# One kernel, four edits: score banks for the last two tiles, a transpose through VectorE and DRAM, a bank order, one clamp

## The chip, the cores and the metric

The kernel is one launch on one core of a Trainium2 chip. The metric is the device time of that launch in microseconds (us), lower is better. The core has five engines that run their own instruction queues in order and wait for each other through semaphores: TensorE (PE, matmuls, with its weight loads listed as PEld), VectorE (DVE), ScalarE (ACT), GpSimd (POOL) and SyncE (SP, which here issues every DMA; its queue is listed as SPq).

## The reference

Attention over pooled queries, then two mixing layers, all in f32:

```
q_pool = mean of neighbouring query rows          # 1152 -> 576 rows, 4 batches x 8 heads, 64 wide
attn   = softmax(q_pool @ k.T / 8);  x = attn @ v  # x: 4 x 576 x 512
xk, xr = mu * x + (1 - mu) * x_prev                # first mixing layer
x      = sigmoid(xr @ w_r) * (relu(xk @ w_k)**2 @ w_v)
theta  = x @ w_theta                               # second mixing layer
y      = w_tok_r @ (x * cos(theta)) + w_tok_i @ (x * sin(theta))
u      = x + y
out    = u + relu(u @ w_ch)
```

A matmul of f32 operands is done in three passes on two rounded parts of each operand (high by high, high by low, low by high; `PASS`). The parts are cut out by ACT (the high one) and by DVE or POOL (the low one).

## The kernel before, in words

The program has three stages, and the order of the instructions on each engine is written out by hand: functions are hung on slots or ticks, and a tick is called after a fixed piece of PE work.

**Attention.** 16 pairs of heads, 9 tiles of 128 query rows each, 144 tiles. A tile's scores fill a set of three PSUM banks; two such sets (`SC`, named sc) take turns. DVE takes the row maximum, ACT the exponential, and then the 128x1152 result must be turned so that keys lie on partitions. For four of nine tiles DVE and DMAs do that; for the others PE transposes nine blocks (`fill`, line 396): one into the third bank of the tile's own scores, four into the bank TX (tx) and four into TY (ty). ACT and DVE copy them out (`take`, line 407). Tiles 7 and 8 of the last pair are the last of the stage and are of that kind. The product with v follows (line 430).

**First mixing layer.** Tokens of all batches are worked in eight halves of 288. `gate` (line 812), `hidden` (line 843) and `value` (line 862) are runs of 48, 96 and 96 matmuls; the gates are done three halves ahead of the others. The shifted inputs are prepared by ACT (line 780), DVE (line 785) and POOL or DVE (line 792). The last five pieces of w_v are converted from f64 while the stage runs (`late_v`, lines 970 to 982): line 970 is the absolute value on ACT, line 972 the clamp on POOL, lines 976 to 978 the bits on DVE, line 982 the low part. `LATE_TICKS` gives for each piece the ticks of its three steps. The results of a matmul run go to PSUM banks in turn; from hidden(6) on, the list `LB` sets which of six banks are taken, starting inside the list where the running count stands: at index 3, which is bank 3, then 5, 7, 0 and so on. `value(5)` has just used banks 4 to 7, and DVE empties them in line 868.

**Second mixing layer.** Tokens are cut into 18 groups of 128 (`angles`; batches 0 and 2 have five, and the fifth holds the last 64 tokens of two batches). Of each group n, `ysplit` (ACT line 1037, POOL line 1038) cuts the two parts of x, `theta(n)` (line 1089) multiplies with w_theta, DVE reduces the angle (lines 1095 to 1104, the last being a clip), ACT makes cosine and sine (1107 to 1109), and `mult` (line 1119, lines 1079 and 1080 for the fifth group) multiplies them with x. For that product x is needed with tokens on partitions, while it is kept with channels on partitions. `turn(n)` makes it: four PE transposes into bank 6 (line 1047) and two ACT copies into the tiles t (line 1050). It is called from `prepare`, inside theta(n-1), four ticks ahead. The products are cut again (lines 1070, 1071) and feed `mix` (line 1143, 108 matmuls per half of 288 tokens), whose result goes through lines 1148, 1150 and 1151 to `final` (line 1162, 48 matmuls). The thetas of batch b+1 are put between the matmuls of mix and final of batch b, at the places of `TPOS`.

Of the kernel before, what the change touches and what calls it, by code (L numbers as in the profile page):

```python
# [11 lines left out]
F32 = mybir.dt.float32  # L12
# [3 lines left out]
ALU = mybir.AluOpType  # L16
# [12 lines left out]
HALF = 288  # L29
WARM = 16  # L30
THIRDS = 6
AHEAD = 3
SHIFT = 33
TURN = 4
TPOS = ((1, 0), (1, 3), (2, 0), (3, 0), (3, 3))
THETA = (1, 2, 4, 5)
YM = (1, 0)
YL = 1
YS = 2
LB = (0, 1, 2, 3, 5, 7)  # L40
PACE = 2.5

CLO = 'pool'
# [4 lines left out]

PIECES = {"a": ((1, 2), ((3, 2), (3, 2), (3, 2)), (9, 2), 14, 15), "x": ((1, 2), ((3, 2), (3, 2), (3, 2)), (4, 2), 6, 7)}
LATE = 5  # L50
LATE_TICKS = ((15, 16, 17), (18, 19, 20), (11, 24, 25), (13, 26, 27), (21, 28, 29))

F64_MIN = float(np.array([0x38000000], np.uint32).view(np.float32)[0])
F64_MAX = float(np.array([0x47EFFFFF], np.uint32).view(np.float32)[0])
# [8 lines left out]
def attn_moe_kernel(ctx: ExitStack, tc: tile.TileContext, qT, kT, vP, muk, mur, wk, wv, wr, wth, wtr, wti, wch, ident, out):  # L63
    nc = tc.nc
    pe, act, dve, pool, sp = nc.tensor, nc.scalar, nc.vector, nc.gpsimd, nc.sync
# [3 lines left out]
    dram = ctx.enter_context(tc.tile_pool(name="dram", bufs=2, space=DRAM))  # L69

    idn = const.tile([128, 128], F32, name="idn")
# [9 lines left out]
    XT = [big.tile([128, 4, 577 + 63 * (1 - b % 2)], F32, name=f"xt{b}") for b in range(NB)]  # L81
# [76 lines left out]
    def attention(first):  # L158
# [11 lines left out]
        TX = psV.tile([128, 512], F32, tag="tx", name="tx")  # L170
# [4 lines left out]
        def bank(eng, ins, *banks):  # L175

            ins = ins.ins
            need = []
            for x in banks:
                e, i = owner.get(x, (eng, None))  # L180
                if e != eng and all(i is not y for y in need):
                    need.append(i)
                owner[x] = (eng, ins)
            for e in ("pe", "act", "dve"):
                if e != eng:
                    tc.declare_no_dep(ins, group="sc_" + e, keep=[i for i in need], reason="ordered bank by bank")
            for i in need:
                tc.add_manual_dep(ins, i.name, sync, reason="bank")
            tc.add_to_no_dep_group("sc_" + eng, ins)
# [197 lines left out]

        FILL = {"o": (8, 9), "y": (0, 4), "x": (4, 8)}

        def fill(n, w):  # L390

            flat = es_[n].rearrange("p a b -> p (a b)")
            k0, k1 = FILL[w]
            ps = {"o": scs[n][:, 2], "x": TX, "y": TY}[w]
            for j, k in enumerate(range(k0, k1)):
                r = pe.transpose(ps[:, 128 * j:128 * j + 128], flat[:, 128 * k:128 * k + 128], idn)  # L396
                if w != "y":
                    bank("pe", r, "tx" if w == "x" else (n % 2, 2))

        def take(n, w):  # L400

            k0, k1 = FILL[w]
            out = erow(n, slice(k0, k1))
            ps = {"o": scs[n][:, 2], "x": TX, "y": TY}[w][:, 0:128 * (k1 - k0)]
            ps = ps.rearrange("p (a b) -> p a b", b=128) if tile_of(n) else ps.rearrange("p (a h b) -> p a h b", h=2, b=64)
            e = "dve" if w == "x" else "act"
            r = (act.copy if e == "act" else dve.tensor_copy)(out, ps)  # L407
            if w != "y":
                bank(e, r, "tx" if w == "x" else (n % 2, 2))

        rest = []

# [301 lines left out]
    def mixtures(WR, nat, cp):  # L714
# [4 lines left out]
        def mem_tile(shape, dt, tag):  # L719
            return (early if tag in EARLY_TAGS else mem).tile(shape, dt, tag=tag, name=tag)  # L720
# [9 lines left out]
        def psum_at(i):  # L730
            return (psm + psn)[i]()
# [32 lines left out]
        def after(n, fn, *args):  # L764
            queue.setdefault(now[0] + n, []).append((fn, args))
# [264 lines left out]
        def ysplit(n, room=None):  # L1030
# [8 lines left out]
                y.append(t)  # L1039
            ys[n] = y  # L1040

        def turn(n):

            b, i = angles[n]
            ps = psum_at(6)
            for k in range(4):
                pe.transpose(ps[:, 128 * k:128 * k + 128], XT[b][:, k, 128 * i:128 * i + 128], idn)
            for a in range(2):
                yt[n, a] = mem_tile([128, HALF], F32, f"t{2 * (n % 2) + a}")
                act.copy(yt[n, a][:, 0:256], ps[:, 256 * a:256 * a + 256])  # L1050

        yt = {}

        def prepare(n):
            if n < len(angles):
                after(TURN, turn, n)
                if n:
                    after(YS, ysplit, n)

# [10 lines left out]
            act.copy(zs[j][0], z)  # L1070
            pool.tensor_tensor(zs[j][1], z, zs[j][0].bitcast(F32), ALU.subtract)

        def tails(yn, q, r):
            for o in range(2):
                z = tile_x(6 - Y0 + o)[:, 0:DM].bitcast(F32)
                c = slice(64 * o, 64 * o + 64)
                for a, y in enumerate(yn):
                    w = slice(256 * a, 256 * a + 256)
                    dve.tensor_tensor(z[0:64, w], y[c, 0:256], q[c, w], ALU.mult)
                    dve.tensor_tensor(z[64:128, w], y[c, 0:256], r[c, w], ALU.mult)  # L1080
                zcut(8 + o, z)

        def theta(n):
            b, i = angles[n]
            y = ys.pop(n)
            ps = psum_at(4)
            for k in range(4):
                for p, (x, w) in enumerate(PASS):
                    pe.matmul(ps, lhsT=y[k // 2][:, k % 2, x], rhs=WT[k][:, w], start=(k == 0 and p == 0), stop=(k == 3 and p == 2))  # L1089
            tick()  # L1090
            qr = tile_q(n % 2).bitcast(F32)
            q, r = qr[:, 0:DM], qr[:, DM:2 * DM]

            def near():
                dve.tensor_scalar(q, ps, float(np.float32(1 / (2 * math.pi))), MAGIC, op0=ALU.mult, op1=ALU.add)
                dve.tensor_scalar(q, q, -MAGIC, 1.0, op0=ALU.add, op1=ALU.mult)
                dve.scalar_tensor_tensor(out=r, in0=q, scalar=-C1, in1=ps, op0=ALU.mult, op1=ALU.add)

            def rest():
                dve.scalar_tensor_tensor(out=r, in0=q, scalar=-C2, in1=r, op0=ALU.mult, op1=ALU.add)  # L1100
                dve.scalar_tensor_tensor(out=r, in0=q, scalar=-C3, in1=r, op0=ALU.mult, op1=ALU.add)

            def clip():
                dve.tensor_scalar(r, r, PI_LO, -PI_LO, op0=ALU.min, op1=ALU.max)  # L1104

            def wave():
                act.activation(q, r, AF.Abs)  # L1107
                act.activation(r, r, AF.Sin)
                act.activation(q, q, AF.Sin, scale=-1.0, bias=hpi)  # L1109

            def mult():
                yn = [yt.pop((n, a)) for a in range(2)]
                if i == 4:
                    tails(yn, q, r)
                    return
                for j, t in ((i, q), (4 + i, r)):
                    for a in range(2):
                        w = slice(256 * a, 256 * a + 256)
                        (dve, pool)[YM[j // 4]].tensor_tensor(t[:, w], yn[a][:, 0:256], t[:, w], ALU.mult)  # L1119
                    zcut(j, t)  # L1120

            near()
            for t, f in zip(THETA, (rest, clip, wave, mult)):
                if t:
                    after(t, f)
                else:
                    f()
            prepare(n + 1)
            tick()

# [58 lines left out]
        n = 5  # L1189
# [61 lines left out]
```

## Time and profile before

| | |
|---|---|
| three runs | 906.19, 907.76, 907.78 us; median 907.76 |
| profiled execution | 906.7 us, of it a span of 904.7 us |
| busy in the span | PE 892.9, DVE 690.8, POOL 590.4, ACT 538.2 us |
| granted TensorE clock | 1.00 over the span |
| DMA | 130.92 MB, of it little after 700 us: 1 GB/s from 710 to 720 us |

"Busy" adds up the time in which an engine had an instruction at work. PE is shown as busy almost throughout, but matmuls overlap at their ends, so how much a run of matmuls costs is read from the starts of the runs, not from the busy sums. The chain of waits is the better guide: it starts at the last instruction and goes back, at each step to what released it.

### The profile page before, as it was taken

How to read it: one execution, taken by the hardware profiler on the slowest of the kernel's cores; microseconds unless marked ns; L12 is line 12 of the kernel's file. 1: busy time of each engine (PE TensorE's matmuls, PEld its weight loads, DVE VectorE, ACT ScalarE, POOL GpSimd, SP SyncE). 2: the span in 40 equal slices, each digit the busy share in tenths (PEclk: the TensorE clock that was granted, in tenths of full speed). 3: DMA queues.
4: the chain of work that ended last, by engine and by line, in shares of the span. 5: the costliest groups of instructions: out<-in, count | busy, mean ns of one | idle time of the engine just before them, and what ended most of it. 6: DMA issues, size and time to landing. Idle time of an engine off the chain costs nothing.

```text
span 904.7 us, 17370 instructions
## 1 busy us (share of the span) xinstructions
PE 892.9 (99%) x6292; PEld 782.4 (86%) x6292; DVE 690.8 (76%) x969; ACT 538.2 (59%) x1131; POOL 590.4 (65%) x656
## 2 busy tenths in 40 slices
PE   8999999999999999999999999999999999999998
PEld 6777777777777777777999999999999999999998
DVE  7988888888988888882798888888668663676612
ACT  8777777777787777764765566565354342443410
POOL 7887777777888687764286656566476574655631
PEclk9999999999999999999999999999999999999999
DMA  7568877777778876669602333334407000010001
GB/s 224 152 186 243 239 204 200 221 216 213 217 216 224 243 231 184 168 165 333 250 2 96 117 98 105 106 109 150 153 26 277 2 28 27 1 54 1 31 23 53
DMA packets 59157, 130.92 MB, mean 145 GB/s; under 512 B 10816, under 2 KB 29952, under 8 KB 59072
## 3 DMA queue, kind: packets, MB, share of 16 engines
q1 hardware_dynamic: 59072, 129.82, 48.5%
q8 instruction: 49, 0.80, 0.4%
q14 instruction: 36, 0.29, 0.1%
HBM read 70.46 MB, written 22.17 MB: 102 GB/s over the span
## 4 chain that ended last, share of the span: by engine, by line
PE 79%; POOL 7%; DMA 4%; issue 4%; DVE 3%; ACT 2%; SPq 1%; POOLq 0%; ACTq 0%; DVEq 0%
PE sc L310 16%; PE ps L1143 13%; PE tx L430 8%; PE ps L862 7%; PE ps L843 7%; PE ty L430 7%; PE ps L1162 6%; PE ps L1089 4%; PE ty L396 3%; PE tx L396 3%; PE ps L812 3%; PE sc L396 2%; POOL k L830 1%; DMA b<-wv 1%; DMA wch<-b 1%
## 5 line engine op out<-in xcount | busy, mean ns | idle before, releaser
L331 DVE TENSOR_REDUCE m<-sc 128x1 f32<-128x1152 f32 x138 | 185.4, 1352 | 46.5 <-PE sc L310 44.1
L343 ACT ACTIVATE e<-sc,m 128x1152 f32<-128x1152 f32 x144 | 176.4, 1225 | 66.1 <-DVE m L331 64.5
L310 PE MATMUL sc<-kt,q 128*128 128x384 f32 (+1 forms) x864 | 188.7, 350 | 2.0 <-ACT E L407 1.0
L310 PEld LDWEIGHTS sc<-kt,q 128*128 128x128 f32 (+1 forms) x864 | 146.0, 189 | 14.3 <-issue 6.4
L1143 PE MATMUL ps<-b,a 128*128 128x288 f32 x816 | 111.2, 295 | 0.0
L1143 PEld LDWEIGHTS ps<-b,a 128*128 128x128 f32 x816 | 109.3, 189 | 0.6
L843 PE MATMUL ps<-x,a 128*128 128x288 f32 x768 | 103.8, 295 | 1.0 <-DVE xt L868 1.0
L862 PE MATMUL ps<-k,b 128*128 128x288 f32 x768 | 103.5, 295 | 0.0
L843 PEld LDWEIGHTS ps<-x,a 128*128 128x128 f32 x768 | 102.3, 188 | 1.3 <-DVE xt L868 1.2
L862 PEld LDWEIGHTS ps<-k,b 128*128 128x128 f32 x768 | 102.0, 188 | 0.3
L201 POOL TENSOR_TENSOR kt<-kn,kh 64x576 fp32r<-64x576 f32 (+1 forms) x64 | 87.6, 1389 | 2.4
L363 DVE STREAM_TRANSPOSE blk<-e 128x1152 f32<-128x1152 f32 x60 | 81.4, 1357 | 0.3 <-DMA wk<-cv 0.3
L430 PE MATMUL tx<-M,vn 128*64 128x320 f32 x540 | 78.5, 435 | 0.0
L830 POOL TENSOR_TENSOR k<-h,k 128x288 fp32r<-128x288 f32 x64 | 58.8, 936 | 21.3 <-ACT k L829 20.8
L476 POOL TENSOR_TENSOR xt<-xt,rb 128x576 f32<-128x576 f32 x16 | 21.9, 1371 | 67.6 <-DMA rb<-scr 43.2
L430 PEld LDWEIGHTS tx<-M,vn 128*64 128x64 f32 x540 | 37.4, 137 | 32.3 <-issue 3.7
L430 PE MATMUL ty<-E,vn 128*64 128x256 f32 x540 | 64.9, 385 | 0.3 <-DMA wk<-cv 0.3
L846 DVE TENSOR_TENSOR h<-h 128x288 f32<-128x288 f32 x64 | 38.5, 603 | 24.7 <-ACT h L845 24.5
L1107 ACT ACTIVATE q<-q 128x512 f32<-128x512 f32 x18 | 11.4, 632 | 77.3 <-DVE q L1104 77.3
L430 PEld LDWEIGHTS ty<-E,vn 128*64 128x64 f32 x540 | 36.4, 136 | 22.8 <-issue 8.0
L407 DVE COPY M<-tx 128x512 f32<-128x512 f32 x80 | 54.5, 681 | 1.8 <-PE tx L396 1.8
L1119 POOL TENSOR_TENSOR q<-t,q 128x256 f32<-128x256 f32 x32 | 24.4, 784 | 47.7 <-ACT q L1109 47.7
(151 smaller groups left out, 1786.8 us busy)
## 6 DMA issues: line engine op xcount, KB each, us to landing
E<-blk SPq DMA_DIRECT2D x240, 144.0 KB
vn<-vP SPq DMA_DIRECT2D x16, 576.0 KB
kn<-kT SPq DMA_DIRECT2D x15, 576.0 KB
qn<-qT SPq DMA_DIRECT2D x15, 576.0 KB
b<-wtk SPq DMA_DIRECT2D x9, 576.0 KB
rb<-scr SPq DMA_DIRECT2D x32, 144.0 KB
out<-xt SPq DMA_DIRECT2D x32, 144.0 KB
cv<-wk SPq DMA_DIRECT2D x8, 512.0 KB
```

The costliest lines, as they stand in the source:

```text
L201: engines[e].tensor_tensor(out, x, hi.bitcast(F32), ALU.subtract)
L310: r = pe.matmul(sc[0:m, c, 0:384], lhsT=x, rhs=k[:, 384 * c:384 * c + 384], start=(i == 0), stop=(i == len(ops) - 1),)
L331: r = dve.tensor_reduce(m, scs[n][:, :, 0:384], axis=AX.XY, op=ALU.max, negate=True)
L343: r = act.activation(e, sc[:, :, 0:384], AF.Exp, bias=m, scale=1.0, accum_out=rss[P][:, t:t + 1])
L363: dve.transpose(out, es_[n].rearrange("p a b -> p (a b)").rearrange("p (k m i) -> p k m i", k=KT, m=4))
L396: r = pe.transpose(ps[:, 128 * j:128 * j + 128], flat[:, 128 * k:128 * k + 128], idn)
L407: r = (act.copy if e == "act" else dve.tensor_copy)(out, ps)
L430: pe.matmul(out, lhsT=vns[P][:, h, j], rhs=e, start=(x == 0), stop=(x == KT - 1))
L830: pool.tensor_tensor(q[:, 1], h, q[:, 0].bitcast(F32), ALU.subtract)
L843: pe.matmul(ps, lhsT=WK[k, f // 4][:, w, 128 * (f % 4):128 * (f % 4) + 128], rhs=x[k][:, c], start=(k == 0 and n == 0), stop=(k == 3 and n ...
L862: pe.matmul(pss[d], lhsT=WV[f][:, w, 128 * d:128 * d + 128], rhs=k2[f][:, c], start=(f == 0 and n == 0), stop=(f == 7 and n == 2))
L1143: pe.matmul(pss[d], lhsT=zs[j][z][:, 128 * d:128 * d + 128], rhs=WTK[min(j, 8)][:, w, cs], start=(m == 0 and n == 0), stop=(m == 8 and n = ...
```

## The change

Four edits.

**Score banks.** For the tiles 7 and 8 of the last pair the four plus four transposes go to the second and first bank of the tile's own scores in place of TX and TY. The copies out of them follow the new places. The count of transposes and copies is the same.

**Turn.** For the groups from n = 5 on (`LOOSE`; 13 of the 18) the four PE transposes and two ACT copies are gone. DVE transposes blocks of 32x32 (two instructions of 128x256), SP stores the two results to a DRAM tile (128 KB each), and after that eight loads of 32 KB bring the blocks to the partitions where they belong. `prepare` calls it two ticks ahead in place of four, counted from theta(n-1). In the t tiles the channels lie in another order, so `mult` and `tails` read and write them through a view with runs of 32.

**Bank order.** `LB` starts with banks 3, 5, 7 in place of 0, 1, 2. The ring is the same, turned by three: index 3 is now bank 0.

**One clamp.** For the last of the late w_v pieces the first step (absolute value on ACT, clamp on POOL) moves from tick 21 to tick 26.

```diff
-LB = (0, 1, 2, 3, 5, 7)
+LB = (3, 5, 7, 0, 1, 2)
...
-LATE_TICKS = ((15, 16, 17), (18, 19, 20), (11, 24, 25), (13, 26, 27), (21, 28, 29))
+LATE_TICKS = ((15, 16, 17), (18, 19, 20), (11, 24, 25), (13, 26, 27), (26, 28, 29))
...
+        def fill_bank(n, w):
+
+            if w == "o" or n >= NT - 2:
+                c = {"o": 2, "x": 1, "y": 0}[w]
+                return scs[n][:, c], (n % 2, c)
+            return (TX, "tx") if w == "x" else (TY, None)
...
-            ps = {"o": scs[n][:, 2], "x": TX, "y": TY}[w]
+            ps, key = fill_bank(n, w)
...
+        def turn_out(n, rooms):
+            b, i = angles[n]
+            d = turned[n] = dram.tile([128, 4, 128], F32, tag="turned", name="turned", bufs=2)
+            for u, t in enumerate(rooms):
+                src = XT[b][:, :, 128 * i + 64 * u:128 * i + 64 * u + 64].rearrange("p k (m j) -> p k m j", m=2)
+                dve.transpose(t.rearrange("p (m k j) -> p k m j", m=2, k=4), src)
+                sp.dma_start(out=d[:, 2 * u:2 * u + 2], in_=t.rearrange("p (m x) -> p m x", m=2))
+
+        def turn_in(n):
+            d = turned.pop(n)
+            for a in range(2):
+                t = yt[n, a] = mem_tile([128, HALF], F32, f"t{2 * (n % 2) + a}")
+                for m in range(4):
+                    sp.dma_start(out=t[32 * m:32 * m + 32, 0:256].rearrange("j (q x) -> j q x", q=2), in_=d.rearrange("(q j) m x -> j q m x", q=4)[:, 2 * a:2 * a + 2, m])
...
+            turn_out(n, [mem_tile([128, HALF], F32, f"h{(2 * n + u) % 3}")[:, 0:256] for u in range(2)])
+            turn_in(n)
...
-                after(TURN, turn, n)
+                after(TURN if n < LOOSE else 2, turn, n)
```

How the instructions stand now is shown at three places. On PE, in the second half of mix of batch 0: ps is the PSUM bank written, idn the identity and xt_70 batch 1's x (a transpose), blk and x the operands of theta(6), b and a those of mix. Before:

```order
L1143 MATMUL ps<-b_8191,a_7715 128x288 x12
L1143 MATMUL ps<-b_8192,a_7883 128x288 x12
L1047 MATMUL ps<-idn,xt_70 128x128 x4
L1089 MATMUL ps<-blk,x_8416 128x512 x6
L1089 MATMUL ps<-blk,x_8419 128x512 x6
L1143 MATMUL ps<-b_8193,a_7888 128x288 x12
L1143 MATMUL ps<-b_8194,a_8062 128x288 x12
L1143 MATMUL ps<-b_8195,a_8067 128x288 x12
L1047 MATMUL ps<-idn,xt_70 128x128 x4
```

Now:

```order
L1180 MATMUL ps<-b_8191,a_7715 128x288 x12
L1180 MATMUL ps<-b_8192,a_7883 128x288 x12
L1126 MATMUL ps<-blk,x_8441 128x512 x6
L1126 MATMUL ps<-blk,x_8444 128x512 x6
L1180 MATMUL ps<-b_8193,a_7888 128x288 x12
L1180 MATMUL ps<-b_8194,a_8062 128x288 x12
```

The transposes of groups 6 and 7 are gone; what stood around them keeps its order.

On DVE, the instructions of theta(5) in the same half of mix: q is the angle tile, the first mult line reads the t tile of group 5. Before:

```order
L1095 TENSOR_SCALAR q_8397<-ps 128x512
L1096 TENSOR_SCALAR q_8397<-q_8397 128x512
L1097 SCALAR_TENSOR_TENSOR q_8397<-q_8397,ps 128x512
L1100 SCALAR_TENSOR_TENSOR q_8397<-q_8397 128x512
L1101 SCALAR_TENSOR_TENSOR q_8397<-q_8397 128x512
L1104 TENSOR_SCALAR q_8397<-q_8397 128x512
L1119 TENSOR_TENSOR q_8397<-t_8271,q_8397 128x256
L1119 TENSOR_TENSOR q_8397<-t_8273,q_8397 128x256
```

Now:

```order
L1132 TENSOR_SCALAR q_8405<-ps 128x512
L1133 TENSOR_SCALAR q_8405<-q_8405 128x512
L1134 SCALAR_TENSOR_TENSOR q_8405<-q_8405,ps 128x512
L1137 SCALAR_TENSOR_TENSOR q_8405<-q_8405 128x512
L1138 SCALAR_TENSOR_TENSOR q_8405<-q_8405 128x512
L1141 TENSOR_SCALAR q_8405<-q_8405 128x512
L1058 STREAM_TRANSPOSE h_8424<-xt_70 128x4x2x32
L1058 STREAM_TRANSPOSE h_8425<-xt_70 128x4x2x32
L1156 TENSOR_TENSOR q_8405<-t_8240,q_8405 128x2x4x32
L1156 TENSOR_TENSOR q_8405<-t_8245,q_8405 128x2x4x32
```

The two block transposes of group 6 (into h tiles) stand between the clip and the products of group 5. The stores of h and the loads of t are issued by SP.

On POOL, in hidden(0) and gate(3): x is the low part that gate(3) reads, k that of value(0), q the late w_v piece, b its low part. Before:

```order
L830 TENSOR_TENSOR k_4919<-h_4888,k_4919 128x288
L972 TENSOR_SCALAR q_4922<-q_4922 128x512
L792 TENSOR_TENSOR x_4925<-t_4873,x_4925 128x288
L830 TENSOR_TENSOR k_4947<-h_4916,k_4947 128x288
L792 TENSOR_TENSOR x_4950<-t_4901,x_4950 128x288
L830 TENSOR_TENSOR k_4970<-h_4944,k_4970 128x288
L792 TENSOR_TENSOR x_4973<-t_4929,x_4973 128x288
L830 TENSOR_TENSOR k_4992<-h_4967,k_4992 128x288
L830 TENSOR_TENSOR k_5014<-h_4989,k_5014 128x288
L982 TENSOR_TENSOR b_5017<-q_4645,b_5017 128x512
L830 TENSOR_TENSOR k_5020<-h_5011,k_5020 128x288
L982 TENSOR_TENSOR b_5056<-q_4645,b_5056 128x512
```

Now:

```order
L839 TENSOR_TENSOR k_4919<-h_4888,k_4919 128x288
L801 TENSOR_TENSOR x_4922<-t_4873,x_4922 128x288
L839 TENSOR_TENSOR k_4944<-h_4916,k_4944 128x288
L801 TENSOR_TENSOR x_4947<-t_4901,x_4947 128x288
L839 TENSOR_TENSOR k_4967<-h_4941,k_4967 128x288
L801 TENSOR_TENSOR x_4970<-t_4926,x_4970 128x288
L839 TENSOR_TENSOR k_4989<-h_4964,k_4989 128x288
L839 TENSOR_TENSOR k_5011<-h_4986,k_5011 128x288
L991 TENSOR_TENSOR b_5014<-q_4645,b_5014 128x512
L839 TENSOR_TENSOR k_5017<-h_5008,k_5017 128x288
L981 TENSOR_SCALAR q_5039<-q_5039 128x512
L991 TENSOR_TENSOR b_5056<-q_4645,b_5056 128x512
```

The clamp (line 972, now 981) has gone behind three of gate(3)'s four x parts and stands ahead of the low part of the seventh w_v piece.

## Rows read from the trace of the kernel before

**Rows 1.** Chain of waits, 395 to 480 us: start, length, what.

```profile
425.26 9.28 DMA b<-wv
...
452.73 0.80 POOL q L972
```

**Rows 2.** Chain of waits, 590 to 700 us.

```profile
599.56 12.30 PE ps L843 x93
...
638.46 2.79 DMA b<-wch
...
690.07 1.15 POOL x L1038
...
698.63 0.44 PE ps L1047 x4
```

**Rows 3.** Groups of instructions, 691 to 905 us: busy, mean ns, idle before.

```profile
L1047 PE MATMUL ps<-idn,xt 128*128 128x128 f32 x52 | 7.8, 272 | 0.0
```

**Rows 4.** Timeline of PE, 630 to 905 us: start, length, line, operation, count.

```profile
738.84 2.96 PE L1089 MATMUL ps<-blk,x 128*128 128x512 f32 x12
...
805.55 3.35 PE L1143 MATMUL ps<-b,a 128*128 128x288 f32 x24
...
820.24 2.95 PE L1089 MATMUL ps<-blk,x 128*128 128x512 f32 x12
...
859.85 12.82 PE L1143 MATMUL ps<-b,a 128*128 128x288 f32 x96
872.51 1.74 PE L1143 MATMUL ps<-b,x 128*128 128x288 f32 x12
874.09 12.94 PE L1143 MATMUL ps<-b,a 128*128 128x288 f32 x96
```

**Rows 5.** Timeline of PE, 409 to 640 us.

```profile
410.52 5.07 PE L430 MATMUL ty<-M,vn 128*64 128x320 f32 x36 [0.24 <-ACT M L407]
...
451.54 2.12 PE L812 MATMUL ps<-x,blk 128*128 128x288 f32 x13
...
460.04 12.80 PE L862 MATMUL ps<-k,b 128*128 128x288 f32 x96
...
624.69 1.74 PE L843 MATMUL ps<-x,a 128*128 128x288 f32 x12
627.43 5.05 PE L843 MATMUL ps<-x,a 128*128 128x288 f32 x36 [0.99 <-DVE xt L868]
```

**Rows 6.** Timeline of all engines, 440 to 482 us.

```profile
451.00 1.07 DVE L785 SCALAR_TENSOR_TENSOR t<-xt,omu,t 128x288 f32<-128x288 f32 x1
...
464.84 0.50 DVE L785 SCALAR_TENSOR_TENSOR t<-xt,omu,t 128x288 f32<-128x288 f32 x1
...
469.44 1.30 POOL L982 TENSOR_TENSOR b<-q,b 128x512 fp32r<-128x512 f32 x1 [1.28 <-ACT b L981]
```

**Rows 7.** Timeline of all engines, 675 to 765 us.

```profile
715.30 0.43 DVE L1104 TENSOR_SCALAR q<-q 128x512 f32<-128x512 f32 x1
...
726.61 0.76 DVE L1119 TENSOR_TENSOR q<-t,q 128x256 f32<-128x256 f32 x2 [1.36 <-ACT q L1108]
...
735.23 2.24 POOL L1038 TENSOR_TENSOR x<-xt,x 128x256 fp32r<-128x256 f32 x2
```

**Rows 8.** Line 455 alone: duration ns min/median/max, first and last start, forms.

```profile
L455 DVE STREAM_TRANSPOSE rt<-r x16: 211/211/214, 40.2 to 414.2; 128x32 f32<-128x32 f32 x16
```

**Rows 9.** Line 363 alone, same columns.

```profile
L363 DVE STREAM_TRANSPOSE blk<-e x60: 1335/1362/1379, 33.2 to 393.6; 128x1152 f32<-128x1152 f32 x60
```

**Rows 10.** Waits of SP's queue: us in total, times, longest.

```profile
SPq L122 <- DMA wtk<-a: 25.8, 18, 2.1
```

**Rows 11.** Line 1165 alone: duration of the issue in ns min/median/max.

```profile
L1165 SPq DMA_DIRECT2D out<-xt x32: 332/333/1311, 737.4 to 901.9; - x32
```

**Rows 12.** Line 372 alone, same columns.

```profile
L372 SPq DMA_DIRECT2D E<-blk x240: 507/590/1649, 44.2 to 407.1; - x120
```

More of the change, by code (lines that the diff above doesn't have):

```diff
@@ L32 @@
 AHEAD = 3
+LOOSE = 5
 SHIFT = 33
@@ L393, in fill @@
             k0, k1 = FILL[w]
-            ps = {"o": scs[n][:, 2], "x": TX, "y": TY}[w]
+            ps, key = fill_bank(n, w)
             for j, k in enumerate(range(k0, k1)):
                 r = pe.transpose(ps[:, 128 * j:128 * j + 128], flat[:, 128 * k:128 * k + 128], idn)
-                if w != "y":
-                    bank("pe", r, "tx" if w == "x" else (n % 2, 2))
+                if key:
+                    bank("pe", r, key)
         def take(n, w):
@@ L403, in take @@
             out = erow(n, slice(k0, k1))
-            ps = {"o": scs[n][:, 2], "x": TX, "y": TY}[w][:, 0:128 * (k1 - k0)]
+            ps, key = fill_bank(n, w)
+            ps = ps[:, 0:128 * (k1 - k0)]
             ps = ps.rearrange("p (a b) -> p a b", b=128) if tile_of(n) else ps.rearrange("p (a h b) -> p a h b", h=2, b=64)
@@ L407, in take @@
             r = (act.copy if e == "act" else dve.tensor_copy)(out, ps)
-            if w != "y":
-                bank(e, r, "tx" if w == "x" else (n % 2, 2))
+            if key:
+                bank(e, r, key)
         rest = []
@@ L1040, in ysplit, with by_quarter, turned_half @@
             ys[n] = y
+        turned = {}
+        def turn_out(n, rooms):
[11 more added lines that the diff above has]
+                    sp.dma_start(out=t[32 * m:32 * m + 32, 0:256].rearrange("j (q x) -> j q x", q=2), in_=d.rearrange("(q j) m x -> j q m x", q=4)[:, 2 * a:2 * a + 2, m])
         def turn(n):
             b, i = angles[n]
[L1045 to L1050, printed above, removed]
+            if n < LOOSE:
+                ps = psum_at(6)
+                for k in range(4):
+                    pe.transpose(ps[:, 128 * k:128 * k + 128], XT[b][:, k, 128 * i:128 * i + 128], idn)
+                for a in range(2):
+                    yt[n, a] = mem_tile([128, HALF], F32, f"t{2 * (n % 2) + a}")
+                    act.copy(yt[n, a][:, 0:256], ps[:, 256 * a:256 * a + 256])
+                return
+            turn_out(n, [mem_tile([128, HALF], F32, f"h{(2 * n + u) % 3}")[:, 0:256] for u in range(2)])
+            turn_in(n)
+        def by_quarter(n, t, a):
+            if n < LOOSE:
+                return t[:, 256 * a:256 * a + 256]
+            return t.rearrange("p (k q j) -> p q k j", k=4, q=4)[:, 2 * a:2 * a + 2]
+        def turned_half(n, t):
+            return t if n < LOOSE else t.rearrange("p (q k j) -> p q k j", q=2, k=4)
         yt = {}
@@ L1071, in zcut, with tails @@
             pool.tensor_tensor(zs[j][1], z, zs[j][0].bitcast(F32), ALU.subtract)
-        def tails(yn, q, r):
+        def tails(n, yn, q, r):
             for o in range(2):
@@ L1077, in tails @@
                 for a, y in enumerate(yn):
-                    w = slice(256 * a, 256 * a + 256)
-                    dve.tensor_tensor(z[0:64, w], y[c, 0:256], q[c, w], ALU.mult)
-                    dve.tensor_tensor(z[64:128, w], y[c, 0:256], r[c, w], ALU.mult)
+                    for d, t in ((slice(0, 64), q), (slice(64, 128), r)):
+                        dve.tensor_tensor(by_quarter(n, z[d], a), turned_half(n, y[c, 0:256]), by_quarter(n, t[c], a), ALU.mult)
                 zcut(8 + o, z)
@@ L1113, in mult @@
                 if i == 4:
-                    tails(yn, q, r)
+                    tails(n, yn, q, r)
                     return
@@ L1117, in mult @@
                     for a in range(2):
-                        w = slice(256 * a, 256 * a + 256)
-                        (dve, pool)[YM[j // 4]].tensor_tensor(t[:, w], yn[a][:, 0:256], t[:, w], ALU.mult)
+                        w = by_quarter(n, t, a)
+                        (dve, pool)[YM[j // 4]].tensor_tensor(w, turned_half(n, yn[a][:, 0:256]), w, ALU.mult)
                     zcut(j, t)
```

## The prediction

> **What bounds the kernel now.** The page's busy line shows PE at work in 99% of the span, and a reader may stop there. Overlapping matmuls make such a sum, so the first view to read is the chain of waits, in order of time, and in it the question which stretches do not lie on PE. There are two that matter here. From 395 us on the chain runs over POOL, a DMA that brings w_v (425.26 to 434.54), ACT, DVE and POOL, with the clamp of line 972 on it, and comes back to PE in gate(3) [rows 1]. From 611.86 (599.56 + 12.30) to 691.22 it runs over conversions, a DMA of w_ch, and the late sequence of DVE, ACT and POOL behind it; it comes back to PE only when POOL ends ysplit(4) [rows 2]. From there to the end it is PE alone. So an edit in the last stretch pays what it takes from PE; one in the two others pays only if it shortens what stands on the chain there. The second view is PE's timeline, for what a group of transposes costs from start to start; the third are timelines of the other engines around the places of the change.
>
> **The change part by part.** Durations are of the profiled execution (906.7 us, of it 904.7 us span; the 2.0 us around it stay).
>
> *Transposes off PE.* In the stretch from 691 us PE does 52 transposes, that is 13 groups of four, all of which go [rows 3]. Their mean of 272 ns is no price, since neighbours overlap: 52 times that would be 14.1 us, while the group's own busy sum is 7.8 us. The chain gives 0.44 us for one group, from its first start to the next matmul's [rows 2]. The timeline confirms it without them: 108 mix matmuls of batch 3 run from 859.85 to 874.09, 14.24 us; the 108 of batch 2 with one group among them from 805.55 to 820.24, 14.69 us; difference 0.45 [rows 4]. 13 x 0.44 = 5.7 us, on the path throughout.
>
> *What replaces them.* DVE gets 26 block transposes of 128x256. Lines 455 and 363 give 0.211 us for 32 columns and 1.362 us for 1152 [rows 8, 9]; on the straight line through both, 256 columns cost 0.211 + 224 x 1.151 / 1120 = 0.44 us, 0.88 us a group. The two stand between the clip of theta(n-1) and its products, where DVE idles 1.36 us for ACT's sine anyway [rows 7], so I cost them at nothing. Without that cover they would be 11.5 us of DVE work beside PE, not on it.
> The way over DRAM has to be done when mult(n) reads t. For the closest pairs, as theta(5) and theta(6), clip(5) ends at 715.73 and mult(6) starts at 726.61: 10.88 us, of which 0.44 go with the transposes between, leaving 10.44 [rows 7]. Needed: two transposes 0.88; issue of the second store 0.33 to 0.59 [rows 11, 12]; its landing 1.43 to 2.1, the mean and the longest wait of line 122 for a store (25.8 us in 18 times) [rows 10]; eight loads at 0.33 to 0.59 each, 2.7 to 4.7; the last one's landing 2.79, which is what 256 KB of w_ch took, here for 32 KB [rows 2]. Sum 8.1 to 11.1 us. I take 9: the DMA engines move next to nothing in this stage, and the short issue is of a store in this same stage. At the far end mult(6) is 0.7 us late. Behind it on DVE and POOL stand the products' cuts, the evacuation of mix and ysplit(8), which ends at 737.47 where theta(8) starts at 738.84 [rows 4, 7]; two removed groups between make 1.37 into 0.49. So 0.7 late would cost PE 0.2 us per close pair, of which there are four (groups 6, 10, 13 and 15); the other nine have more time. Taken: 0, bounds 0 to 0.8.
> The products' new view costs nothing that I can see: same elements, runs of 32. If POOL took twice as long over it, its waits for ACT before the products would not cover it, but ysplit has the slack above and more.
>
> *Score banks.* PE stands idle before the last product with v for 0.24 us, for ACT's copy of the last tile, which had queued behind the one of the tile before [rows 5]. With two tiles in this position the saving is at most 0.48. But the next thing that PE waits for is not ahead of it: w_v lands at 434.54 whatever PE did [rows 1], ACT and DVE go on from there, and gate(3) waits for POOL. Taken: 0, bounds 0 to 0.5.
>
> *The clamp.* Gate(3), 48 matmuls, takes from 451.54 to 460.04, 8.50 us [rows 5], where 48 at 0.132 us (96 in 12.66 us [rows 4]) take 6.33. It waits for its x parts, and the 0.80 us of the clamp stand between the first and the second [rows 1]. Taking it away gives at most 0.8. What is late next: value(0) starts at 460.04 and comes to its eighth block, the last w_v piece, 84 matmuls later, at 471.12; POOL ends that piece at 470.74 (469.44 + 1.30) [rows 5, 6]. Only 0.38 us of slack, and the clamp now stands ahead of this piece. If the piece ends when it did, PE wins 0.38; if the clamp delays it by its own length, PE loses 0.42. Taken: +0.4, bounds -0.4 to +0.8.
> Rows speak on this: line 785 of DVE takes 1.07 us at 451.00 with POOL at work beside it, 0.50 at 464.84 [rows 6]. The Trainium skill, page "SBUF — State Buffer", section "SBUF: two separate sides", says that VectorE with two SBUF inputs and GpSimd lock a shared port pair for a whole instruction, so that the other one stands still. By that rule the clamp costs DVE its length wherever it is put, and DVE has no idle time up to the last piece: the gain would be the slack alone or less, and the sum 5.7 us; by the row before the edit and its 0.38, 6.1.
>
> *Bank order.* hidden(6)'s second block waits for a bank that DVE has not emptied: twelve matmuls from 624.69 would end at 626.27, the next starts at 627.43, 1.16 us lost [rows 5]. The new order takes banks 0 to 2 there, long free. PE is then 1.16 us ahead, and waits that much more at theta(4), since the chain up to ysplit(4) hangs on the w_ch load that lands at 641.25 [rows 2], not on PE. Taken: 0, bounds 0 to 1.16.
>
> *Sum.* 5.7 + 0.4 = 6.1 us. The profiled execution of 906.7 lies inside the runs, 1.06 below their median of 907.76; I forecast against the median: 901.7 us.
>
> **The rivals.**
> *The early edits pay too.* If the sequence up to theta(4) moves with PE after all: 5.7 + 0.8 + 1.16 + 0.5 = 8.2 us, 899.6 us. For it: DVE and POOL have short idle times in those stretches. Against: the chain names no PE in them. 8%.
> *The turn is somewhat late.* 12 us for the way over DRAM put mult 1.56 us late at the four close pairs, PE loses about 1.1 each: 4.3 us, 906.0 us. 9%.
> *The turn is much late, and the kernel slower.* DVE and POOL wait in order on t, everything behind them waits too, and the thetas run dry. It decides from 12.9 us: 2.46 late, 1.97 lost at each of four pairs, 7.9 us in all, which is the gain and 1.8 more. At 13.5 us it is 10.3 us, 912.0 us. For it: the issue of one such DMA took up to 1.65 us [rows 12], and eight loads follow each other. Against: an idle DMA system in this stage. 8%.
> The Trainium skill, page "VectorE: DVE Perf Modes", section "Rules for kernel authors", speaks for this rival: for 128x128 it sends a transpose to TensorE where PSUM will do. No run here shows yet which is right in a stage where PE alone sets the end.
>
> **How the numbers follow.** Forecast 75%, the three rivals 8, 9 and 8%. A difference of about 0.2% (1.8 us) is what a measurement of this kernel can tell from none. Faster than that: the forecast, the first rival and half of the second, 88%; within it: 5%; slower 7%. The likeliest case alone spans 900.9 (clamp +0.8 with some of the banks) to 902.9 (clamp -0.4, turn 0.8 late). The range to 8 in 10 reaches into the first and the second rival: 899.8 to 905.0; the third is left out.
>
> **What would show it.** Right: no transpose on PE behind 707 us, and PE's mix and final runs gapless there, each batch shorter by 4 or 5 times 0.44; DVE's block transposes near 0.44 us; mult waiting for ACT, not for a DMA; t landing 8 to 11 us after clip. gate(3) shorter by 0.4 to 0.8; no wait at hidden(6) and one of about 1.5 us at theta(4) (or at theta(3)) for POOL. Wrong: waits of line 1119's successor on t's DMA, thetas waiting for ysplit, or a wait in value(0) for its last piece longer than gate(3) gained.

## The result, and the profile after

| | kernel before | changed kernel | ratio (95% interval) |
|---|---|---|---|
| first comparison | 907.77 us (906.19 to 908.25, 4 runs) | 899.67 us (898.99 to 899.85, 4 runs) | 0.9912 (0.9895 to 0.9930) |
| second (e5) | 906.0 us (9 runs) | 899.88 us (5 runs) | 0.9933 (0.9920 to 0.9945) |
| third (e15) | 906.02 us (21 runs) | 900.13 us (5 runs) | 0.9932 (0.9918 to 0.9945) |

Faster, as forecast, by more than forecast in the first comparison (8.1 us where 6.1 stood) and by just the forecast's sum in the two later ones (6.1 and 5.9). The predicted 901.7 us was 2.0 too high, and 899.67 lies 0.13 us below the range. The gain came from the place where it was looked for; two terms were too small, one was given back, and the level from which the sum was subtracted was too high.

The profiled execution of the changed kernel took 899.7 us, with a span of 897.9. Its lines are 1 (early) to 37 (late) higher than those of the kernel before: gate is line 821, hidden 852, value 871, theta 1126, mix 1180, ysplit 1046 and 1047, PE's turn 1074, DVE's block transpose 1058.

PE's timeline of the changed kernel up to theta(4), against [rows 5] (start, length, line, operation, count, idle before):

```profile
451.24 7.89 PE L821 MATMUL ps<-x,blk 128*128 128x288 f32 x48
458.96 11.46 PE L871 MATMUL ps<-k,b 128*128 128x288 f32 x86
470.77 1.59 PE L871 MATMUL ps<-k,b 128*128 128x288 f32 x10 [0.35 <-POOL b L991]
...
624.56 6.50 PE L852 MATMUL ps<-x,a 128*128 128x288 f32 x48
...
689.97 2.59 PE L1126 MATMUL ps<-blk,x 128*128 128x512 f32 x10 [0.24 <-POOL x L1047]
692.40 14.42 PE L1180 MATMUL ps<-b,a 128*128 128x288 f32 x108
```

gate(3) takes 7.72 us to the next start in place of 8.50; value(0) now waits for its last piece; hidden(6) runs through; theta(4) still waits 0.24 us for POOL, although PE got there 1.3 us earlier. The chain of waits shows what theta(4) waits for, against [rows 2]:

```profile
629.96 7.05 DMA wch<-b
637.08 2.89 DMA b<-wch
...
688.77 1.16 POOL x L1047
689.97 2.59 PE ps L1126 x10
```

The same chain, but the load of w_ch that landed at 641.25 lands at 639.97. Behind theta(4), first PE in the run of batch 2 that answers to [rows 4], then DVE and SP for group 6:

```profile
800.21 14.40 PE L1180 MATMUL ps<-b,a 128*128 128x288 f32 x108
814.46 2.96 PE L1126 MATMUL ps<-blk,x 128*128 128x512 f32 x12
```

```profile
713.22 0.43 DVE L1141 TENSOR_SCALAR q<-q 128x512 f32<-128x512 f32 x1
713.56 0.77 DVE L1058 STREAM_TRANSPOSE h<-xt 128x256 f32<-128x256 f32 x2
...
714.02 1.13 SPq L1059 DMA_DIRECT2D turned<-h  x2
...
716.12 4.46 SPq L1066 DMA_DIRECT2D t<-turned  x8
...
724.02 0.76 DVE L1156 TENSOR_TENSOR q<-t,q 128x256 f32<-128x256 f32 x2 [0.69 <-ACT q L1145]
```

The 108 matmuls take 14.25 us in place of 14.69. The block transposes stand behind the clip and ahead of the sine's end; the eight loads are issued by 720.58; the products start at 724.02 and wait for ACT, not for a DMA.

One table carries the rest of this document. It cuts PE's timeline of every profile but e11's at the same seven starts: the last pair's first product with v (395 to 398 us), gate(0), gate(3), hidden(1), hidden(6), the first mix, and the last run of nine matmuls. Each number is the difference of two starts, in us; the tail is from that last start to the end of the span.

| stretch | kernel before (4 profiles: first, e1, e13, e14) | changed (3: first, e5, e15) | single edits |
|---|---|---|---|
| to gate(0) | 22.90 to 22.92 | 22.53 to 22.55 | |
| gate(0) to gate(3) | 32.13 to 32.82 | 32.18 to 32.41 | |
| gate(3) to hidden(1) | 21.03 to 21.15 | 20.70 to 20.95 | clamp alone 20.72 |
| hidden(1) to hidden(6) | 152.01 | 152.22 to 152.37 | clamp alone 152.26 |
| hidden(6) to mix | 68.29 to 69.02 | 67.84 to 68.40 | bank order alone 68.28; all but the turn 67.05 |
| mix to last run | 206.27 to 206.29 | 200.48 to 200.49 | turn alone 200.49 |
| tail | 4.70 to 4.74 | 5.01 to 5.09 | turn alone 5.00 |

### The profile page after: what moved, and what is told of

Same layout as the page of the kernel before. It is cut to its first block, busy times and chain, and to the rows that moved or that the text cites. A ratio compares the mean times of both kernels' runs of the same rounds, so it can differ in the third digit from the quotient of the medians.

```text
span 897.9 us, 17527 instructions
## 1 busy us (share of the span) xinstructions
PE 887.5 (99%) x6240; PEld 778.9 (87%) x6240; DVE 697.2 (78%) x995; ACT 531.0 (59%) x1105; POOL 591.0 (66%) x656
## 4 chain that ended last, share of the span: by engine, by line
PE 38%; DVE 4%; POOL 3%; issue 3%; ACT 1%; DMA 1%; POOLq 0%; ACTq 0%; SPq 0%; DVEq 0%
PE ps L1180 13%; PE ps L852 7%; PE ps L871 6%; PE ps L1199 6%; PE ps L1126 4%; PE ps L821 3%; POOL k L839 1%; DMA wch<-b 1%; POOL x L1047 1%; POOL a L1109 1%; DVE h L855 1%; POOL q L1156 0%; DVE t L794 0%; DVE q L986 0%; DVE q L985 0%
## 5 line engine op out<-in xcount | busy, mean ns | idle before, releaser
L1109 POOL TENSOR_TENSOR a<-q,a 128x512 fp32r<-128x512 f32 x32 | 45.9, 1457 | 11.7 <-ACT a L1108 11.7
L801 POOL TENSOR_TENSOR x<-t,x 128x288 fp32r<-128x288 f32 x52 | 44.6, 878 | 13.6 <-ACT x L800 13.5
```

## The experiments

Where a run is timed, its median stands beside that of the kernel before on the same chip in the same hour: 905.69 us (27 runs) for e1 to e4, 906.0 (9) for e5 to e8, 907.21 (17) for e9 to e12, 906.02 (21) for e13 to e16.

### The kernels unchanged: e1, e13, e14 and e5, e15

e1, the kernel before. 

> The kernel before, unchanged, for a second profile. Theory A (the bank order pays what PE waits in hidden(6), and that wait differs from execution to execution): 906 to 908.3 us, and if this profiled execution is slower than 906.7, PE's idle time before the second block of hidden(6) is longer than the 0.99 us of the first profile by about as much. Theory B (the spread of before has nothing to do with that wait): the wait stays at 0.9 to 1.1 us whatever the time.

e5, the changed kernel. 

> The changed kernel, unchanged, timed beside the kernel before on the chip and in the hour of the other experiments. If the 8.1 us of the first comparison are the change: 897.6 us, 8 below the kernel before. If 1 to 2 us of them were the kernel before in a run of slow executions (the first profile had a w_ch load that was issued 1.7 us later than in the second profile): 899 to 900 us, 6 to 6.7 below.

e13 and e14, the kernel before. 

> The kernel before, for a third profile. Theory A (its level is set by when the last b<-wch load is issued, since theta(4)'s third matmul starts 52.85 us behind that issue or with PE's own time if that is later): time = 268 us + the issue where the issue is 638 or later, e.g. 906.7 at 638.5, and about 905.5 with an issue below 637. Theory B (the start of gate(0), 418.4 to 419.9 so far, sets the level): the time follows that start and not the issue.

> The same for a fourth profile. Theory A and theory B as for the third.

e15, the changed kernel. 

> The changed kernel beside the kernel before for the third time. If it shares the levels of the kernel before: 6.1 us below it again, 899.7 to 901.1 us with a kernel before of 905.8 to 907.2. If the bank order frees it of the slow executions: 899.7 to 900.0 whatever the kernel before shows, ratio 0.992 where that is at 907 or above, 0.9933 where it is at 906.

Measured: e1 905.5, e13 905.85, e14 905.58 (0.9994 to 0.9997 of the kernel before, intervals with 1 in them), e5 and e15 as in the table above. PE's timeline of e1 around hidden(6) and theta(4):

```profile
624.36 1.74 PE L843 MATMUL ps<-x,a 128*128 128x288 f32 x12
627.10 5.05 PE L843 MATMUL ps<-x,a 128*128 128x288 f32 x36 [0.99 <-DVE xt L868]
...
689.92 2.95 PE L1089 MATMUL ps<-blk,x 128*128 128x512 f32 x12
692.71 4.92 PE L1143 MATMUL ps<-b,a 128*128 128x288 f32 x36
```

SP's issues of the last load of w_ch, in e1 and then in e4 (below):

```profile
636.72 0.33 SPq L122 DMA_DIRECT2D b<-wch  x1
```

```profile
636.06 0.33 SPq L123 DMA_DIRECT2D b<-wch  x1
```

The wait in hidden(6) is the same 0.99 us, so theory A of e1 falls: that wait does not vary. But theta(4) has no wait here. The last load of w_ch was issued at 636.72, not at 638.46, and so ysplit(4) was ready before PE came. So my first profile, on which the forecast rests, was a late case in this point. Theory A of e13 is half right: hidden(6) to mix takes 69.02 us with the late load and 68.29 to 68.35 without, 0.7 us. The rest of the spread follows the start of gate(0) in its order, 418.38 in e1, 419.42 in e14, 420.10 in e13 (profiled executions 905.5, 906.06 and 906.57), as theory B has it; in size it follows the start of gate(3), 451.20, 451.82 and 452.29. None of the profiled executions of the kernel before is above 906.7, so what makes the kernel before take 907.8 and more is not seen in any profile and stays open.

e5 and e15: the changed kernel stands at 899.9 and 900.1 beside 906.0, 6.1 and 5.9 us below. The extra 2 us of the first comparison are the kernel before at 907.77, while the changed kernel stays between 898.74 and 900.43 in all 14 runs of the three comparisons. Whether the edits also spare it the runs above 907 that the kernel before has is not shown: it was not timed in the hour of 907.21. e10, which differs from it by one ysplit, was 8.0 us below the kernel before in that hour, and 7.3 below in e16, timed beside e15.

### The turn: e4, e6, e8, e11

e4, with `LOOSE = 18` (no group turned by DVE):

```diff
-LOOSE = 5
+LOOSE = 18
```

> The changed kernel with all 18 groups turned by PE again (LOOSE = 18), the three other edits kept. By both theories the turn is worth what the stretch behind theta(4) shortened by in the profile, 5.5 us: 905.2 us (904.9 to 905.5). If the turn also disturbs or helps something ahead of theta(4), it differs from that by more than 0.5.

e6, the kernel before with the turn alone, here as a difference to the changed kernel:

```diff
-LB = (3, 5, 7, 0, 1, 2)
+LB = (0, 1, 2, 3, 5, 7)
-LATE_TICKS = (..., (26, 28, 29))
+LATE_TICKS = (..., (21, 28, 29))
-            if w == "o" or n >= NT - 2:
+            if w == "o":
```

> The kernel before with the turn of 13 groups alone. By the sum: 5.5 us (5.3 to 5.9) below the kernel before, 0.9939. If the three other edits are what makes room for it: less than 5.

Measured: e4 905.24, ratio 0.9994 (0.9985 to 1.0002); e6 900.05, ratio 0.9937 (0.9924 to 0.9949). The turn is the change: 5.95 us of it by e6; the three other edits together give 0.45, not distinguishable from nothing. In the profiles PE's time from mix to the last run falls from 206.28 to 200.49 in every kernel with the turn of 13 groups, 5.79 us or 13 x 0.445. The two starts, first of the kernel before and then of e6:

```profile
693.71 4.92 PE L1143 MATMUL ps<-b,a 128*128 128x288 f32 x36
...
900.00 1.35 PE L1162 MATMUL ps<-k,g 128*128 128x288 f32 x9
```

```profile
693.21 7.04 PE L1180 MATMUL ps<-b,a 128*128 128x288 f32 x52
...
893.70 1.35 PE L1199 MATMUL ps<-k,g 128*128 128x288 f32 x9
```

Of the 5.79 us, 0.3 come back in the tail.

e8, each load of t in two:

```diff
-    sp.dma_start(out=t[32 * m:32 * m + 32, 0:256]..., in_=...[:, 2 * a:2 * a + 2, m])
+    for q in range(2):
+        sp.dma_start(out=t[32 * m:32 * m + 32, 128 * q:128 * q + 128], in_=...[:, 2 * a + q, m])
```

> The changed kernel with every load of t split in two (16 loads of 16 KB per group in place of 8 of 32 KB): eight more issues of 0.42 us, so the way over DRAM takes about 3.4 us longer, 12.4 us against the 10.4 that the four closest pairs have. My third rival's price (0.79 us for each us that mult is late, at four pairs): mult about 2 us late, 6 us in all, 905 to 906 us. Theory B (DVE and POOL wait, but catch up before a theta or mix needs them): below 1 us, 899 to 900.5 us.

Measured: 899.64, ratio 0.9932 (0.9918 to 0.9945), like the changed kernel. The waits of DVE and of POOL from 692 to 900 us (engine, tile, line, what was waited for: us in total, times, longest):

```profile
DVE q L1157 <- DMA t<-turned: 6.3, 5, 1.6
```

```profile
POOL q L1157 <- DMA t<-turned: 5.2, 6, 3.3
```

Now t is late, as intended, by up to 1.6 us on DVE and 3.3 on POOL, and PE notices nothing: mix to last run 200.49. The price of my second and third rivals, the lateness less 0.49 us at each close pair, makes 1.1 us of the longest wait of DVE alone; it is wrong where it was to apply.

e11, groups 1 to 4 as well:

```diff
-LOOSE = 5
+LOOSE = 1
```

> The changed kernel with the groups 1 to 4 turned by DVE and DRAM too (LOOSE = 1): 16 transposes off PE between hidden(6) and theta(4). If PE set that stretch: 4 x 0.42 = 1.7 us won, 898.1 us. By the later of two times (PE's own, or the late sequence behind the w_ch load): PE is earlier and waits more at theta(3) and theta(4), and the eight block transposes lengthen DVE's part: 0 to 2 us slower, 899.9 to 901.9 us. Its 32 loads also stand on SP's queue between the stores and loads of w_ch, which would make the last b<-wch load later than 637.3.

Measured: 910.28, ratio 1.0036 (1.0024 to 1.0049), slower than either theory. PE's timeline, and the waits of SP's queue from 640 to 700 us:

```profile
672.81 6.05 PE L871 MATMUL ps<-k,b 128*128 128x288 f32 x42 [1.70 <-ACT h L854]
680.36 3.04 PE L1126 MATMUL ps<-blk,x 128*128 128x512 f32 x12 [1.51 <-DVE q L1134]
...
690.88 2.60 PE L1126 MATMUL ps<-blk,x 128*128 128x512 f32 x10 [0.66 <-POOL x L1047]
...
700.83 4.45 PE L1180 MATMUL ps<-b,a 128*128 128x288 f32 x17 [7.34 <-DMA b<-wtk]
```

```profile
SPq L1059 <- DVE h L1058: 27.0, 4, 14.7
```

The waits at theta(3) and theta(4) grew as expected, but they are the small part. SP issues in order; its stores of turned blocks wait 27.0 us for DVE, and behind them stand the nine loads of w_tok that mix needs. They were issued from 649.9 to 689.4 us in e5 and from 696.93 to 701.55 here:

```profile
696.93 4.62 SPq L1222 DMA_DIRECT2D b<-wtk  x9
```

The wait of 7.34 us also cost PE its clock. The granted clock is 0.50, the 1.2 GHz level, from 700.8 to 705.2 us, and the run of 108 matmuls takes 16.71 us to the next start in place of 14.25: 2.46 us more. From mix to the last run e11 takes 202.95 us, by just these 2.46 more than 200.49. So the turn pays behind the last of these loads, and costs ahead of it.

### The bank order: e2, e3

e2, the kernel before with the bank order alone; e3, the changed kernel without it:

```diff
-LB = (0, 1, 2, 3, 5, 7)
+LB = (3, 5, 7, 0, 1, 2)
```

> The kernel before with the new bank order alone. Theory A (PE sets the way up to theta(4), through the angles of theta(2) and theta(3)): hidden(6) runs without a wait, theta(4) comes as much earlier, its wait stays near 0.25 us, 1.2 us or more are won: 905.5 to 906.6 us. Theory B (my forecast: the w_ch load that lands at 641.25 sets theta(4)): the wait moves to theta(4), which starts at 691.2 as before, 907.5 to 907.8 us.

> The changed kernel with the old bank order. Theory A: the wait in hidden(6) is back, about 1.2 to 2.2 us slower, 900.9 to 901.9 us. Theory B: no slower, 899.5 to 899.9 us.

Measured: e2 904.83, ratio 0.9988 (0.9980 to 0.9997), 0.9 us won; e3 900.07, ratio 0.9936 (0.9922 to 0.9950), within noise of e5's 899.88. PE's timeline of e2:

```profile
624.60 6.50 PE L843 MATMUL ps<-x,a 128*128 128x288 f32 x48
...
679.91 3.02 PE L1089 MATMUL ps<-blk,x 128*128 128x512 f32 x12 [0.45 <-DVE q L1097]
...
690.44 2.60 PE L1089 MATMUL ps<-blk,x 128*128 128x512 f32 x10 [0.25 <-POOL x L1038]
```

Neither theory holds alone. The wait goes and part of it comes back at theta(3) and theta(4): hidden(6) to mix is 68.28. In e4 the load was issued at 636.06 and nothing came back: 67.05. Over the six profiles with the new order and nothing else moved there (first, e2, e4, e5, e8, e15) the mean is 67.94, over the seven with the old one (first, e1, e3, e6, e12, e13, e14) 68.48: 0.54 us of the 1.16 stay. The two sets overlap (67.05 to 68.40 and 68.00 to 69.02), so this mean is good to about 0.5 either way, and the timed differences of e2, e3 and e4 (0.9, 0.2 and 0.45) do not settle it. The rule that fits: POOL starts ysplit(4) 51.6 to 52.4 us behind the issue of that last load in 13 of the 15 profiles in which it has its old place and LOOSE is not 1 (the two others are e7 and e9, below), while PE, where nothing holds it up, reaches theta(4) 64.3 us after the start of hidden(6) (e4), or 65.2 to 65.7 with the old bank order; the later of the two decides. The issue itself came 11.6 to 13.8 us after the start of hidden(6), by chance as far as these runs show.

### The load that theta(4) waits for: e7, e9, e10

e7, the four loads of w_theta, 2 MB in all, ahead of value(4) in place of ahead of hidden(6):

```diff
+            if (f, i) == (value, 4):
+                WT = block_tile(F32R)
+                WT = [pair(WT[:, k, 0:1024]) for k in range(4)]
+                for k in range(4):
+                    sp.dma_start(out=WT[k].bitcast(F32), in_=WD["wth", k])
             f(i)
```

> The changed kernel with the four loads of w_theta (blk, 512 KB each) issued ahead of value(4) in place of ahead of hidden(6). Theory A (theta(4) starts at the later of two times: PE's own, 64.3 us after the start of hidden(6), and 52.8 us after the issue of the last b<-wch load; that load waits for a store that stands behind the four loads): the b<-wch load is issued at 634 or earlier, theta(3) and theta(4) have no wait left, 0.3 to 1.0 us below the changed kernel. Theory B (PE alone sets theta(4)): no change within 0.2 us. If the four loads only jam the queue 40 us earlier, waits appear between 587 and 625 instead and it is slower.

e9, the same place, but one load every six ticks:

```diff
-                    sp.dma_start(out=WT[k].bitcast(F32), in_=WD["wth", k])
+                    after(6 * k + 1, lambda k=k: sp.dma_start(out=WT[k].bitcast(F32), in_=WD["wth", k]))
```

> The changed kernel with the four loads of w_theta issued one at a time, six ticks apart, from the start of value(4) on, in place of all four ahead of hidden(6). Theory A (the pieces of w_ch go in a ring load, convert, store, load; 2 MB in one lump holds up a store by 7 us, wherever the lump stands; the ring hands this on to ACT and DVE, which wait in order, and so to PE): without a lump the last b<-wch load is issued before 633, PE has no wait left from hidden(6) to theta(4), mix of batch 0 starts 67.1 us after hidden(6) (67.8 to 68.2 in the changed kernel), 0.7 to 1.1 us won: 898.8 to 899.2 us. Theory B (the late sequence of ACT, DVE and POOL needs its time whatever the loads do): 67.8 to 68.2 as before, 899.6 to 899.9 us.

Measured: e7 901.91, ratio 0.9959 (0.9947 to 0.9972); e9 902.66, ratio 0.9950 (0.9937 to 0.9964); e7 2.0 us slower than e5 beside it, e9 with a ratio that is worse than all three of the changed kernel's; hidden(6) to mix takes 70.14 and 70.71 us, where the changed kernel has 67.84 to 68.40. Timelines of e7, then of e9:

```profile
631.76 0.66 PE L1075 MATMUL ps<-idn,xt 128*128 128x128 f32 x4 [1.75 <-DVE xt L877]
...
635.38 0.33 SPq L123 DMA_DIRECT2D b<-wch  x1
```

```profile
637.10 0.33 SPq L123 DMA_DIRECT2D b<-wch  x1
...
643.57 5.38 PE L871 MATMUL ps<-k,b 128*128 128x288 f32 x27 [1.83 <-ACT h L854]
```

Theory A fails in both. In e7 the last load came 1.7 us earlier (635.38), but the b<-wch load before it moved from 619.43 to 623.17; DVE, which works in order, emptied value(5)'s banks that much later, and PE waited 1.75 us elsewhere. In e9 the last load did not move at all. Behind the wait of 1.83 us its granted clock is 0.73 from 643.5 to 645.5 us and 0.53 to 648, and the 27 matmuls take 5.22 us to the next start where 3.6 is their time in the changed kernel: 1.6 us of what e9 loses are the clock's. The 2 MB cost the ring of load, convert, store its time wherever they stand: from one b<-wch load to the next it took 12.6 and then 17.7 us in the changed kernel (606.88, 619.43, 637.08), 14.5 and 14.4 in e9, 10.7 and 12.2 in e7, but there from a start 5.6 us later (612.49).

e10 and e16, ysplit(4) two ticks into value(7), ahead of the products of group 2 on POOL:

```diff
-        value(7, {3: lambda: theta(3)})
+        value(7, {1: lambda: ysplit(4), 3: lambda: theta(3)})
```

> The changed kernel with ysplit(4) called two ticks into value(7), ahead of the products of group 2 on POOL in place of behind their cut. Theory A (what theta(4) waits for is POOL's place in its order, 3 us of cuts ahead of ysplit(4)): the wait at theta(4), 0.25 us by the profile and 0.5 us from start to start, is gone, 899.2 to 899.6 us; a wait at theta(3) of 0.3 us, which is for DVE, may stay. Theory B (PE alone): no change, 899.7 to 899.9 us. If the cut of group 2 comes too late for mix instead, a new wait of up to 2 us.

> The changed kernel with ysplit(4) early, beside the changed kernel on one chip. Theory A: 0.2 to 0.5 us below it. Theory B: within 0.2 us of it.

Measured: e10 899.21, ratio 0.9916 (0.9902 to 0.9929); e16 898.74, ratio 0.9927 (0.9914 to 0.9939), beside e15's 900.13. PE's timeline of e10:

```profile
681.47 3.04 PE L1126 MATMUL ps<-blk,x 128*128 128x512 f32 x12 [0.85 <-DVE q L1134]
...
691.13 2.96 PE L1126 MATMUL ps<-blk,x 128*128 128x512 f32 x12
```

The wait at theta(4) is gone in both profiles, the one at theta(3) stays, as theory A has it. But hidden(6) to mix is no shorter in them, 68.65 and 68.05 us, and both profiled executions (901.24 and 901.34) are the longest of their runs, so they do not show where the lower medians come from. It is the fastest version by its median in e16, but the intervals of e15 and e16 overlap: a lead that these runs do not prove.

### The clamp: e12

The kernel before with the clamp moved alone:

```diff
-LATE_TICKS = (..., (21, 28, 29))
+LATE_TICKS = (..., (26, 28, 29))
```

> The kernel before with the clamp moved alone. By my forecast's term 0.4 us from gate(3)'s start to the start of hidden(1): 20.7 us in place of 21.1, with gate(3) shorter by 0.8 and 0.4 given back in value(0) before its last piece. Of this less than 0.4 arrives at hidden(6), since the new kernels so far took 0.2 to 0.35 us longer from hidden(1) to hidden(6) (152.2 to 152.4 us in place of 152.0). In time 905.5 to 906.0 us, no difference that can be measured.

Measured: 906.66, ratio 0.9998 (0.9988 to 1.0007). gate(3) to hidden(1) 20.72 us, 0.39 less; hidden(1) to hidden(6) 152.26, 0.25 more. The timelines of e5 say where that goes (PEld is the weight load); POOL starts the x parts behind the last w_v piece at the same 470.69 as in the kernel before:

```profile
470.69 6.60 POOL L801 TENSOR_TENSOR x<-t,x 128x288 fp32r<-128x288 f32 x7
470.78 1.36 PEld L871 LDWEIGHTS ps<-k,b 128*128 128x128 f32 x10 [0.30 <-POOL b L991]
473.62 11.40 PEld L852 LDWEIGHTS ps<-x,a 128*128 128x128 f32 x86 [0.17 <-POOL x L801]
```

PE comes earlier to hidden(1), and hidden(1)'s inputs do not. In e12 itself the weight load waits 0.3 us in hidden(1), there for an x part that DVE makes.

## Why the prediction was wrong, point by point

*The step that failed* is "The profiled execution of 906.7 lies inside the runs, 1.06 below their median of 907.76; I forecast against the median: 901.7 us". Three runs between 906.2 and 907.8 were taken as the kernel's level. The later medians of the same kernel are 905.69, 906.0, 907.21 and 906.02, those of the changed one 899.67, 899.88 and 900.13. From the profiled execution the same sum gives 900.6; from 906.0 it gives 899.9, which was measured. The range had no room for an error of the level. Why the kernel before ran above 907 in the first comparison is open, as said above. The upper end of the likeliest case, 902.9, is also a slip: clamp -0.4 and the turn 0.8 late make 901.7 + 0.8 + 0.8 = 903.3.

*Turn.* Right: 5.7 us forecast, 5.79 measured on PE. The block transposes took 0.416 us where 0.44 was estimated, beside ACT's sine, at no cost. The way over DRAM was in time, and e8 shows that it need not have been: the cover is larger than the 10.44 us that I worked out, since DVE and POOL are late without PE being late. I had priced the waits behind mult with ysplit(8)'s 1.37 us of slack alone. The rule that I cited from the Trainium skill, page "VectorE: DVE Perf Modes", section "Rules for kernel authors", would keep these transposes on PE; in this stage, where PE alone sets the end, e6 with DVE's is 6 us faster. The tail's 0.3 us was not foreseen.

*Clamp.* The mechanism and its size were right in their place: 0.4 taken, 0.39 measured, with the wait at value(0)'s last piece that was named. The step fails one run of matmuls later: hidden(1) and what follows give 0.2 to 0.36 us back. The forecast stopped at the last w_v piece and did not ask what POOL and DVE do behind it. The other price that stood beside it, a gain of the slack alone or less and 5.7 us in all, did not come: gate(3) to hidden(1) is 20.64 to 20.95 us in every profile with the edit and 21.03 to 21.15 in every one without.

*Banks.* Taken at 0, measured 0.37 us up to gate(0) (bound 0.5), 22.89 to 22.92 us in the profiles without the edit and 22.52 to 22.55 in those with it. The reason given, a w_v load that lands when it lands, did not show: gate(0) to gate(3) takes 32.1 to 32.9 us with the edit and without, a spread in which no give-back of 0.37 can be seen.

*Bank order.* Taken at 0, measured 0.54 on average. The chain was read rightly: in the first profile theta(4) hung on the w_ch load. What failed is to take the load's time of one execution for a constant. The wait of about 1.5 us that I expected at theta(4) was 0.24 us, since the load came 1.3 us earlier in the second profile. With the early load of e4 PE is the later one, and there the edit pays in full.

Put together: 0.37 + (0.37 - 0.31) + 0.54 + 5.79 - 0.36 = 6.4 us, with the means of the table's stretches over all kernels that have the edit or lack it (the tail without e8 and e11); 5.9 and 6.1 were timed. That 6.1 was the forecast's sum too is in part luck: the terms that it put at nothing, 0.37 and 0.54, and the tail's -0.36 that it did not have, come to 0.55, and the clamp fell 0.34 short. The first rival had 899.6 us for "the early edits pay too"; it meets the measured time, but not for its reason: of the 2.1 us that it has more than the forecast, about 0.6 came.

## What to carry to other kernels

Where PE alone sets the end of a stage, four transposes are worth their distance from start to start, and a way round over an idle DMA system may be late without harm as long as the engines that wait for it have slack of their own. A wait in one profile that ends on a DMA is one draw; take a second profile before calling the DMA's time fixed, and give the level of the kernel before a range of its own. An instruction moved ahead on an in-order engine is only worth what the next thing on the same engine lets PE keep. A wait of PE can cost more than its length, when the clock falls behind it.

## What the runs showed of the hardware

- The wait from the last DVE instruction to the end of the span, in which the last store runs, is 2.78 us in the kernel before (901.46 + 0.46 to 904.7) and 3.10 in the changed one (894.34 + 0.46 to 897.9). All kernels with 13 groups turned by eight loads each have the longer tail (5.00 to 5.15 us in the table's measure); e8 with sixteen loads has the short one (4.71), and so has e11 with 17 groups by eight (4.72). The cause is open. The last DVE instruction before, then now:

```profile
901.46 0.46 DVE L1164 SCALAR_TENSOR_TENSOR xt<-ps,xt 128x288 f32<-128x288 f32 x1 [1.12 <-PE ps L1162]
```

```profile
894.34 0.46 DVE L1201 SCALAR_TENSOR_TENSOR xt<-ps,xt 128x288 f32<-128x288 f32 x1 [1.12 <-PE ps L1199]
```

- Loads of 32 KB from DRAM took 0.418 us to issue in the median, 0.303 to 1.73 us at the ends, in e5; with sixteen of 16 KB the median of one is the same, 0.419, so the halves cost twice the issue (min/median/max in ns, e5 and then e8):

```profile
L1066 SPq DMA_DIRECT2D t<-turned x104: 303/418/1732, 701.3 to 848.5; - x104
```

```profile
L1067 SPq DMA_DIRECT2D t<-turned x208: 302/419/1542, 701.2 to 853.6; - x104
```

- A store of 128 KB, issued right behind 2 MB of loads, needed 7.05 us until the load that waited for it could go on, in the chain of the changed kernel.
- After a wait of PE the granted clock fell in two runs and not in a third. Behind 7.34 us (e11) it was 0.50 from 700.8 to 705.2 us and 0.74 to 707, behind 1.83 us (e9) 0.73 and then 0.53 from 643.5 to 648, behind 1.75 us (e7) 1.00. It cost 2.46 us on 108 matmuls and 1.6 us on 27. What decides is not shown.
